# A Fourier filter and a mixture of experts on one core: rows due later, halves that go when their sums are made, w2 of the short tiles loaded along more tiles

## The chip, the cores and the metric

The kernel runs on one core of a Trainium2 chip. The metric is the device time of one execution in microseconds (us), as the median of several runs. A core has five engines, each with an instruction queue of its own: TensorE (PE in the profile) for matrix products, VectorE (DVE), ScalarE (ACT), GpSimd (POOL), and SyncE (SP), which here issues most DMA transfers. Every engine works through its own list in the order in which the program wrote it, and waits at an instruction whose input another engine or a transfer hasn't delivered.

## The reference

Two blocks, one after the other. The first filters every channel of a sequence in the frequency domain; the second sends each row to the one expert of eight that its gate prefers.

```python
# x: (8, 2496, 256); filt_r, filt_i: (1249, 256)
X = np.fft.rfft(x, axis=1)
y = np.fft.irfft(X * (filt_r + 1j * filt_i)[None], n=2496, axis=1)

x = y.reshape(19968, 256)
logits = x @ w_gate                        # (19968, 8)
expert = argmax(logits, axis=1)
gate = probability of that expert (softmax)
for e in range(8):                         # w1: (8, 256, 1024), w2: (8, 1024, 256)
    rows = rows whose expert is e
    out[rows] = gate[rows] * (relu(x[rows] @ w1[e]) @ w2[e])
```

## The kernel before

The Fourier transform of length 2496 = 39 x 64 is done as matrix products in four steps per batch (a and b forward, c and d back, with the filter between b and c). Between a and b the data goes through DRAM (`zd`), and between c and d again (`ud`). After d come the gate's logits, the routing, and a scatter of every row into a list of its expert in DRAM (`rows`). A tile of 512, 256 or 128 rows of one expert is then read back (`xg`), transposed (`xT`), multiplied by w1, passed through relu, multiplied by w2, scaled by the gate and scattered to the output.

The tiles of experts from earlier batches are worked on between the Fourier steps of later ones; after the last batch only expert tiles remain. Which step goes next is decided once, when the program is written, by a model of the time: `now` is TensorE's model time, `free` the time at which each other engine is thought free, `when` the time at which something is counted as there.

Loads are queued ahead:

```python
def prefetch():
    i = got["x"]
    if i < len(work) and rows_at[work[i][3]] <= now[0] and i - used["x"] < 2:
        rows_in(i)
        when["x", i] = now[0] + 6.0
        got["x"] += 1
    for what in ("w1", "w2"):
        h = got[what]
        if h < 2 * len(work) and rows_at[work[h // 2][3]] <= now[0] and (
                h - used[what] < ((3 if what == "w1" else 2) if h < 2 * SHORT else 8)):
            weights(h, what == "w2")
            when[what, h] = now[0] + 7.0
            got[what] += 1
    for h in range(used["w1"], got["w1"]):
        if quarters(h // 2) and h not in wsum and len(wsum) < 2 and when["w1", h] <= now[0]:
            w1_sums(h)
```

The first product of a tile (with w1) is done in two halves `h`. For tiles of 512 rows, and those of 256 rows of the last batch, a half is done with seven block products in place of eight, which need sums of blocks of the rows (`sums`, one set per tile) and of blocks of w1 (`wsum`, one set per half), both made by GpSimd:

```python
def turn_x(i):
    ...  # transposes of the rows, copies out of PSUM
    if quarters(i):
        ...  # four gpsimd.tensor_tensor over sums
        free["p"] = max(free["p"], now[0]) + 0.75 * n

def w1_sums(h):
    ...  # four gpsimd.tensor_tensor over wsum
    free["p"] = max(free["p"], now[0]) + 3.0

def hidden_by_quarters(h):
    ...
    q = product(w[:, 0, 0], b[:, 0, 0])      # no sums
    ...
    q = product(w[:, 1, 0], b[:, 1, 0])      # no sums
    add(hT[:, 0, :, 0], q, part)
    yield 1.71
    q = product(ws[:, 1], t[:, 1])           # sums of both kinds from here on
    ...
```

The steps of the expert tiles, each with its TensorE time and the thing it needs:

```python
def half(h):
    i, g = divmod(h, 2)
    n = TILES[i][0]
    if quarters(i):
        if h not in wsum:
            yield lambda: w1_sums(h), 0.0, ("w1", h)
        steps = hidden_by_quarters(h)
        for t in (1.71, 1.71, 1.71, 0.85):
            yield lambda: next(steps), t * n / 4, ("w1", h)
        wsum.pop(h)
    else:
        for a in range(4):
            yield lambda: hidden(i, g, a), 0.43 * n, ("w1", h)
    ...

def due(what, i):
    return when.get((what, i), now[0] + 1.0) <= now[0]

for i in range(NT):
    ahead = i > 0 and (used["x"] > i or due("x", i)) and due("w1", 2 * i)
    if i > 0 and not ahead:
        yield from results(i - 1)
    yield from turned(i)
    yield from half(2 * i)
    if i + 1 < NT and due("x", i + 1):
        yield from turned(i + 1)
    if ahead:
        yield from results(i - 1)
    yield from half(2 * i + 1)
```

And the loop that chooses between the next Fourier step `f` and the next expert step `e`:

```python
asked = e and e[2] in when
halt = f and f[2] and (f[2][0] in "uy" and held_y[0] == YB)
late_in = f and f[2] and lands.get(f[2], 0.0) > now[0]
if e and asked and (not f and not sides or
        when[e[2]] <= now[0] and (credit > 0.0 or not f or halt or late_in)):
    e[0]()                                   # the expert step
    ...
elif f and not halt and (not f[2] or f[2] == "y" or f[2] in ins):
    f[1]()                                   # the Fourier step
    ...
else:
    now[0] += 1.0
```

`late_in` says that the Fourier step's input is counted as still on its way; `f[2] in ins` only that its load has been queued.

The short tiles of 128 rows at the end take w2 of all eight experts from SBUF (`w2s`, 16 loads of 512 KB). `late` exists once the last Fourier step and the last routing are written:

```python
def weights(h, second):
    i, k = divmod(h, 2)
    if late and second and TILES[i][1] == B - 1 and late["n"] < 2 * E:
        e, hf = divmod(late["n"], 2)
        nc.sync.dma_start(out=late["w2s"][:, e, hf * FH2:(hf + 1) * FH2], in_=moe_w2[e, hf])
        late["n"] += 1
    if second and i >= SHORT:
        return
    ...  # the load of w1 or w2 of this tile
```

Of the kernel before, what the change touches and what calls it, by code (L numbers as in the profile page):

```python
# [22 lines left out]
E = 8  # L23
# [95 lines left out]
def kernel(  # L119
# [18 lines left out]
    B = x.shape[0]  # L138
# [73 lines left out]
    now = [0.0]  # L212
# [475 lines left out]
    late = {}  # L688
# [19 lines left out]
    def weights(h, second):  # L708

        i, k = divmod(h, 2)  # L710
        if late and second and TILES[i][1] == B - 1 and late["n"] < 2 * E:

            e, hf = divmod(late["n"], 2)
            nc.sync.dma_start(out=late["w2s"][:, e, hf * FH2:(hf + 1) * FH2], in_=moe_w2[e, hf])
# [3 lines that stand above are left out]
        ev = nc.sync.value_load(work[i][1], min_val=0, max_val=E - 1)  # L718
        if second:
            w2t[h] = pools["moe"].tile([P, FH2, D], F32, tag="w2t", name="w2t", bufs=2)  # L720
            nc.sync.dma_start(out=w2t[h], in_=moe_w2[bass.ds(ev, 1), k].rearrange("o p i d -> p (o i) d"))
        else:
            pool, bufs = (late["w1"], 8) if i >= SHORT else (pools["moe"], 3)
            w1t[h] = pool.tile([P, DH, 2, 2 * P], F32, tag="w1t", name="w1t", bufs=bufs)
            nc.sync.dma_start(out=w1t[h], in_=moe_w1[bass.ds(ev, 1), k].rearrange("o p i h f -> p (o i) h f"))

    def turn_x(i):
        n, xg = work[i][0], xgs.pop(i)
        idt[i] = pools["moe"].tile([P, 4, 1], I32, tag="idt", name="idt", bufs=3)
        gts[i] = pools["moe"].tile([P, 4, 1], F32, tag="gts", name="gts", bufs=3)  # L730
        nc.vector.tensor_copy(idt[i][:, :n], xg.bitcast(I32)[:, :n, D:D + 1])  # L731
        nc.vector.tensor_copy(gts[i][:, :n], xg[:, :n, D + 8:D + 9])
        xts[i] = pools["moe"].tile([P, DH, 4 * P], F32, tag="xT", name="xT", bufs=2)
        for dh in range(DH):
            pt = bank().rearrange("p (i q) -> p i q", i=4)
            for j in range(n):
                nc.tensor.transpose(pt[:, j, :], xg[:, j, dh * P:(dh + 1) * P], ident)  # L737
            evac(xts[i][:, dh, :n * P].rearrange("p (j q) -> p j q", j=n), pt[:, :n], n * P)
        if quarters(i):

            b = xts[i][:, :, :n * P].rearrange("p h (r c) -> p h r c", r=2)
            t = sums[i] = pools["moe"].tile([P, 4, 2 * P], F32, tag="sums", name="sums", bufs=2)[:, :, :n * HP]
            nc.gpsimd.tensor_tensor(t[:, 0], b[:, 0, 1], b[:, 0, 0], op=ALU.subtract)
            nc.gpsimd.tensor_tensor(t[:, 1], b[:, 1, 1], t[:, 0], op=ALU.subtract)
            nc.gpsimd.tensor_tensor(t[:, 2], b[:, 1, 1], b[:, 0, 1], op=ALU.subtract)
            nc.gpsimd.tensor_tensor(t[:, 3], b[:, 1, 0], t[:, 1], op=ALU.subtract)
            free["p"] = max(free["p"], now[0]) + 0.75 * n

    def w1_sums(h):

        w = w1t[h]
        t = wsum[h] = pools["moe"].tile([P, 4, 2 * P], F32, tag="wsum", name="wsum", bufs=2)
        nc.gpsimd.tensor_tensor(t[:, 0], w[:, 0, 1], w[:, 1, 1], op=ALU.add)  # L753
        nc.gpsimd.tensor_tensor(t[:, 1], t[:, 0], w[:, 0, 0], op=ALU.subtract)  # L754
        nc.gpsimd.tensor_tensor(t[:, 2], w[:, 0, 0], w[:, 0, 1], op=ALU.subtract)
        nc.gpsimd.tensor_tensor(t[:, 3], w[:, 1, 0], t[:, 1], op=ALU.subtract)
        free["p"] = max(free["p"], now[0]) + 3.0

    def hidden_by_quarters(h):

        i = h // 2
        w, ws, t = w1t[h], wsum[h], sums[i]
        n = work[i][0]
        b = xts[i][:, :, :n * P].rearrange("p h (r c) -> p h r c", r=2)
        hT = pools["moe"].tile([P, 2, 2, 4 * P], F32, tag="hT", name="hT", bufs=3)
        hs.setdefault(i, []).append(hT)  # L770
        hT = hT[:, :, :, :n * P].rearrange("p f v (r c) -> p f v r c", r=2)

        def product(left, right):
            q = bank()[:, :n * P].rearrange("p (v c) -> p v c", v=2)
            for v in range(2):
                mm(q[:, v], lhsT=left[:, v * P:(v + 1) * P], rhs=right, start=True, stop=True)  # L776
            return q

        def add(o, q, a):
            nc.vector.tensor_tensor(o, q, a, op=ALU.add)  # L780
            free["v"] = max(free["v"], now[0]) + 0.15 + 0.14 * n

        def relu(o, q):
            nc.scalar.activation(o.rearrange("p v r c -> p v (r c)"), q.rearrange("p v r c -> p v (r c)"), AF.Relu)  # L784
            free["s"] = max(free["s"], now[0]) + 0.2 + 0.22 * n

        low, part = hT[:, 1, :, 0], hT[:, 0, :, 1]
        q = product(w[:, 0, 0], b[:, 0, 0])
        nc.scalar.copy(out=part, in_=q)  # L789
        free["s"] = max(free["s"], now[0]) + 0.6  # L790
        q = product(w[:, 1, 0], b[:, 1, 0])
        add(hT[:, 0, :, 0], q, part)
        yield 1.71
        q = product(ws[:, 1], t[:, 1])
        add(part, q, part)
        q = product(ws[:, 2], t[:, 2])
        add(low, q, part)
        yield 1.71
        q = product(ws[:, 0], t[:, 0])
        add(hT[:, 1, :, 1], q, low)  # L800
        add(part, q, part)
        q = product(w[:, 1, 1], t[:, 3])
        add(low, q, low)
        relu(hT[:, 1], hT[:, 1])
        yield 1.71
        q = product(ws[:, 3], b[:, 1, 1])
        add(part, q, part)
        relu(hT[:, 0], hT[:, 0])
        yield 0.85
# [139 lines left out]
    def prefetch():  # L949

        i = got["x"]
        if i < len(work) and rows_at[work[i][3]] <= now[0] and i - used["x"] < 2:
            rows_in(i)
            when["x", i] = now[0] + 6.0
            got["x"] += 1
        for what in ("w1", "w2"):
            h = got[what]
# [9 lines that stand above are left out]
    def experts():  # L967

        def turned(i):
            if used["x"] == i:
                yield lambda: turn_x(i), 0.22 * TILES[i][0], ("x", i)
                used["x"] += 1
# [4 lines that stand above are left out]
            if quarters(i):  # L980
                if h not in wsum:
                    yield lambda: w1_sums(h), 0.0, ("w1", h)
                steps = hidden_by_quarters(h)
                for t in (1.71, 1.71, 1.71, 0.85):
                    yield lambda: next(steps), t * n / 4, ("w1", h)
                wsum.pop(h)
            else:
                for a in range(4):
                    yield lambda: hidden(i, g, a), 0.43 * n, ("w1", h)
            w1t.pop(h)  # L990
            used["w1"] += 1
            if g:
                xts.pop(i), sums.pop(i, None)

        def due(what, i):
            return when.get((what, i), now[0] + 1.0) <= now[0]

        def results(i):
            for j in range(TILES[i][0]):
                yield lambda: result(i, j), 3.42, ("w2", 2 * i + 1)  # L1000
            hs.pop(i), idt.pop(i), gts.pop(i), w2t.pop(2 * i, None), w2t.pop(2 * i + 1, None)
            used["w2"] += 2
# [12 lines that stand above are left out]
        yield from results(NT - 1)  # L1015
# [77 lines left out]
```

## Time and profile before

| | |
|---|---|
| time, median of 3 runs | 1587.04 us (1583.56 to 1589.24) |
| span of the profiled run | 1582.1 us, mean granted TensorE clock 0.989 |
| VectorE, ScalarE, GpSimd busy | 47%, 33%, 42% of the span |
| moved by DMA | 287.55 MB, 182 GB/s over the span |
| chain that ended last | TensorE 71%, DMA 11%, issue 8%, VectorE 4%, GpSimd 4% |
| w1 loads (512 KB), issue to landing | 3.7 us median, 130 of them |
| w2 loads (512 KB), issue to landing | 4.2 us median, 84 of them |
| Fourier inputs from `zd` (256 KB) | 9.2 us median, 70 of them |

In the profile L776 is the product by quarters (`product`), L817 the plain first product (`hidden`), L834 the second product (`result`), L737 the transposes of the rows (`turn_x`). L337, L351, L372 and L391 are the Fourier steps a, b, c and d, L358 to L362 the filter on VectorE between b and c, L743 to L746 the sums of the rows and L753 to L756 those of w1. `fin` is any Fourier input, `bank` a PSUM bank. A line of the waits names the engine, what it was about to do, what it waited for, the total in us, how often, and the longest. The profile's slices are 40 equal parts of the span, with the busy share in tenths.

### The profile page before, as it was taken

What the parts mean: (1) busy time and instruction counts of PE and PEld (TensorE: products, weight loads), DVE (VectorE), ACT (ScalarE), POOL (GpSimd) and SP (SyncE); (2) the same over time, 40 slices, a digit from 0 to 9 for tenths busy, and PEclk for the clock granted to TensorE, in tenths of its full rate; (3) what the DMA queues carried; (4) which work ended last, traced back from release to release, by engine and by line L of the source; (5) the groups of instructions that cost most, each with busy time, mean ns of one, the idle gap of its engine ahead of it and who ended that gap; (6) DMA issues with size and microseconds to landing.
All of it is one profiled execution on the core that took longest, in us unless ns stands there. A gap on an engine that the chain in (4) does not pass through costs nothing.

```text
span 1582.1 us, 24007 instructions
## 1 busy us (share of the span) xinstructions
PE 1519.9 (96%) x7624; PEld 1207.6 (76%) x7624; DVE 748.4 (47%) x1923; ACT 524.1 (33%) x1074; POOL 669.5 (42%) x817
## 2 busy tenths in 40 slices
PE   7989797999989999999999999999999999989998
PEld 5534456767668868787688788888888898989997
DVE  4675574544745565456645455564343434420000
ACT  4434342333333233233233332322232323223433
POOL 4132135324544454365345636646455546621111
PEclk9999898999999999999999999999999999999999
DMA  8669796697675477365733734443345456565560
GB/s 244 167 189 274 251 299 221 183 313 234 200 240 154 162 224 213 104 178 149 201 109 127 214 104 121 128 146 124 116 170 172 151 172 227 184 234 178 175 186 32
DMA packets 119281, 287.55 MB, mean 182 GB/s; under 512 B 17587, under 2 KB 58812, under 8 KB 119157
## 3 DMA queue, kind: packets, MB, share of 16 engines
q1 hardware_dynamic: 99941, 242.69, 51.3%
q0 software_dynamic: 19216, 43.33, 7.8%
q8 instruction: 63, 1.03, 0.3%
q14 instruction: 61, 0.50, 0.1%
HBM read 205.95 MB, written 80.90 MB: 181 GB/s over the span
## 4 chain that ended last, share of the span: by engine, by line
PE 71%; DMA 11%; issue 8%; DVE 4%; POOL 4%; ACT 1%; POOLq 0%; SPq 0%; ACTq 0%; DVEq 0%
PE bank L834 28%; PE bank L776 20%; DMA out_dram<-ys,idt 6%; PE bank L391 4%; PE bank L351 3%; PE bank L372 3%; PE bank L337 3%; PE bank L817 3%; DMA zd<-zo 2%; PE bank L466 2%; PE bank L737 2%; PE lt L480 1%; DVE hT L780 1%; DMA fin<-ud 1%; PE bank L413 1%
## 5 line engine op out<-in xcount | busy, mean ns | idle before, releaser
L834 PE MATMUL bank<-w2t,hT 128*128 128x256 f32 x2240 | 500.9, 381 | 5.4 <-DMA w2t<-in_moe_w_dram 4.3
L834 PEld LDWEIGHTS bank<-w2t,hT 128*128 128x128 f32 x2240 | 422.3, 191 | 78.6 <-issue 18.6
L780 DVE TENSOR_TENSOR hT<-bank,hT 128x512 f32<-128x512 f32 (+1 forms) x504 | 299.1, 626 | 287.2 <-PE bank L776 202.9
L840 POOL DMA_INDIRECT out_dram<-ys,idt x163 | 161.7, 992 | 505.0 <-ACT ys L839 242.0
L607 POOL DMA_INDIRECT rows<-yo,row x176 | 174.4, 991 | 178.0 <-DVE row L577 47.2
L784 ACT ACTIVATE hT<-hT 128x1024 f32<-128x1024 f32 (+1 forms) x144 | 133.0, 957 | 339.6 <-DVE hT L780 339.6
L839 ACT ACTIVATE ys<-bank,gts 128x256 f32<-128x256 f32 x159 | 75.2, 475 | 416.4 <-PE bank L834 361.3
L776 PE MATMUL bank<-sums,wsum 128*128 128x256 f32 (+1 forms) x864 | 186.7, 363 | 11.2 <-POOL wsum L754 8.3
L776 PEld LDWEIGHTS bank<-sums,wsum 128*128 128x128 f32 x864 | 151.3, 194 | 40.7 <-POOL wsum L754 10.1
L817 PE MATMUL bank<-xT,w1t 128*128 128x128 f32 (+1 forms) x928 | 134.5, 299 | 2.3 <-ACT zo L227 1.4
L817 PEld LDWEIGHTS bank<-xT,w1t 128*128 128x128 f32 x928 | 123.0, 193 | 18.0 <-issue 8.2
L776 PE MATMUL bank<-xT,w1t 128*128 128x256 f32 (+1 forms) x576 | 123.2, 357 | 0.0
L776 PEld LDWEIGHTS bank<-xT,w1t 128*128 128x128 f32 x576 | 100.7, 190 | 16.2 <-issue 4.1
L731 DVE COPY idt<-xg 128x4 int32<-128x4 int32 (+2 forms) x65 | 19.3, 297 | 176.2 <-DMA out_dram<-ys,idt 143.0
L753 POOL TENSOR_TENSOR wsum<-w1t 128x256 f32<-128x256 f32 x73 | 53.7, 735 | 111.2 <-PE bank L776 90.6
L358 DVE TENSOR_TENSOR ys<-bank,ht 128x512 f32<-128x512 f32 x80 | 54.9, 686 | 91.7 <-PE bank L351 91.3
L823 ACT ACTIVATE hT<-bank 128x128 f32<-128x128 f32 (+1 forms) x230 | 68.0, 299 | 52.1 <-PE bank L817 46.4
L834 PE MATMUL bank<-w2s,hT 128*128 x368 | 83.2, 379 | 0.0
L372 PE MATMUL bank<-ys,tcs 128*128 128x512 f32 x140 | 75.2, 620 | 8.1 <-DVE ys L362 7.9
L337 PE MATMUL bank<-fin,tas 117*120 117x512 f32 x154 | 75.1, 606 | 0.4 <-ACT hT L789 0.4
L834 PEld LDWEIGHTS bank<-w2s,hT 128*128 128x128 f32 x368 | 68.1, 190 | 8.3
L351 PE MATMUL bank<-fin,tbs 128*128 128x512 f32 x140 | 73.1, 603 | 0.0
(149 smaller groups left out, 1754.9 us busy)
## 6 DMA issues: line engine op xcount, KB each, us to landing
w1t<-in_moe_w_dram SPq DMA_DIRECT2D x130, 512.0 KB, 3.7
w2t<-in_moe_w_dram SPq DMA_DIRECT2D x84, 512.0 KB, 4.2
fin<-in_x_dram SPq DMA_DIRECT2D x40, 512.0 KB, 9.4
fin<-zd SPq DMA_DIRECT2D x70, 256.0 KB, 9.2
ud<-uo SPq DMA_DIRECT2D x70, 256.0 KB, 4.6
zd<-zo SPq DMA_DIRECT2D x35, 480.0 KB, 10.1
fin<-ud SPq DMA_DIRECT2D x35, 480.0 KB, 9.6
xg<-rows SPq DMA_DIRECT2D x28, 544.0 KB, 3.6
```

Source lines behind the costliest of these rows:

```text
L337: mm(p[:TK, :], lhsT=tas, rhs=xt[:TP, j:j + 2, :], start=True, stop=True)
L351: mm(p, lhsT=tbs, rhs=zi[:, j:j + 2, :], start=True, stop=True)
L372: mm(p, lhsT=tcs, rhs=ys, start=True, stop=True)
L607: sc = nc.gpsimd.indirect_dma_start(out=rowsd, out_offset=bass.IndirectOffsetOnAxis(ap=at, axis=0), in_=what, in_offset=None,)
L776: mm(q[:, v], lhsT=left[:, v * P:(v + 1) * P], rhs=right, start=True, stop=True)
L780: nc.vector.tensor_tensor(o, q, a, op=ALU.add)
L784: nc.scalar.activation(o.rearrange("p v r c -> p v (r c)"), q.rearrange("p v r c -> p v (r c)"), AF.Relu)
L817: mm(p[:, :m], lhsT=w1t[2 * i + g][:, dh, fh, v * P:(v + 1) * P], rhs=xts[i][:, dh, :m], start=(dh == 0), stop=(dh == DH - 1))
L823: lambda: nc.scalar.activation(hT, p[:, :m], AF.Relu))
L834: mm(p[:, :D], lhsT=hs[i][k % 4 // 2][:, k // 4, k % 2, j * P:(j + 1) * P], rhs=w2, start=(k == 0), stop=(k == FT - 1))
L839: lambda: nc.scalar.activation(ys, p[:, :D], AF.Copy, scale=gate))
L840: nc.gpsimd.indirect_dma_start(out=out, out_offset=bass.IndirectOffsetOnAxis(ap=idt[i].bitcast(U32)[:, j, :], axis=0), in_=ys, in_offset=None,
```

## The change

Four numbers and conditions of the model change; no operation is added or removed. Rows are counted as there 9 us after their load is queued and not 6, so later than w1 with its 7. The sums of rows and of w1 get a time at which they are counted as made (`when["sums", i]`, `when["wsum", h]`), and all steps of a half by quarters wait in the model for both, where they waited for w1 alone. And the loads of `w2s` go along with the w2 loads of any tile once `late` exists, not only those of the last batch, so that they are spread over an earlier stretch. The aim is an order in which TensorE does not come to an operand before it is there.

```diff
-        if late and second and TILES[i][1] == B - 1 and late["n"] < 2 * E:
+        if late and second and late["n"] < 2 * E:
...
-            free["p"] = max(free["p"], now[0]) + 0.75 * n
+            free["p"] = max(free["p"], now[0] + 1.0) + 0.75 * n
+            when["sums", i] = free["p"] + 1.0
... (w1_sums)
         free["p"] = max(free["p"], now[0]) + 3.0
+        when["wsum", h] = free["p"] + 1.0
... (prefetch)
-            when["x", i] = now[0] + 6.0
+            when["x", i] = now[0] + 9.0
... (half)
+                when["quarters", h] = max(when["sums", i], when["wsum", h])
                 steps = hidden_by_quarters(h)
                 for t in (1.71, 1.71, 1.71, 0.85):
-                    yield lambda: next(steps), t * n / 4, ("w1", h)
+                    yield lambda: next(steps), t * n / 4, ("quarters", h)
```

## The prediction

> **What bounds the kernel now.** I read the totals first, then the busy shares by slice, then the list of what TensorE waited for, and last the timelines around the longest waits.
>
> ```profile
> span 1582.1 us, 24007 instructions
> PE 1519.9 (96%) x7624; PEld 1207.6 (76%) x7624; DVE 748.4 (47%) x1923; ACT 524.1 (33%) x1074; POOL 669.5 (42%) x817
> PE   7989797999989999999999999999999999989998
> PEclk9999898999999999999999999999999999999999
> ```
>
> TensorE is the bound: 96% busy, nobody else over half. The change adds and removes no matmul, so only TensorE's idle time (1582.1 - 1519.9 = 62 us) and its half-rate clock can give anything. Both sit in the first quarter. The waits of TensorE name what stops it:
>
> ```profile
> PE bank L737 <- DMA xg<-rows: 9.6, 2, 5.6
> PE bank L776 <- POOL wsum L754: 8.3, 2, 5.1
> PE bank L372 <- DVE ys L362: 7.9, 7, 3.6
> ...
> PE bank L834 <- DMA w2t<-in_moe_w_dram: 4.3, 2, 3.4
> ```
>
> The change is aimed at four of these: rows 9.6, weight sums 8.3, row sums (further down the list) 1.8, w2 4.3, together 24.0 us. In time they are: rows 5.6 us at 172.7 to 178.3 (first 256-row tile) and 4.0 us at 452.5; weight sums at 242 and 257 (first 512-row tile); row sums at 1342 and 1357; w2 at 1388 to 1394. The timeline of TensorE at the weight sums (the bracket is the idle time before a group):
>
> ```profile
> 240.37 1.99 PE L776 MATMUL bank<-xT,w1t 128*128 128x256 f32 x8
> 247.49 5.34 PE L776 MATMUL bank<-sums,wsum 128*128 128x256 f32 x12 [5.13 <-POOL wsum L754]
> ...
> 259.93 4.26 PE L776 MATMUL bank<-sums,wsum 128*128 128x256 f32 x12 [3.19 <-POOL wsum L754]
> ...
> 265.75 3.62 PE L817 MATMUL bank<-xT,w1t 128*128 128x256 f32 x16
> ```
>
> and the queue of SyncE beside it:
>
> ```profile
> 234.38 0.38 SPq L698 DMA_DIRECT2D xg<-rows  x1
> ...
> 241.78 1.00 SPq L300 DMA_DIRECT2D zd<-zo  x2
> 247.56 0.47 SPq L322 DMA_DIRECT2D fin<-zd  x1
> 248.09 0.59 SPq L323 DMA_DIRECT2D fin<-zd  x1
> 248.73 1.06 SPq L317 DMA_DIRECT2D fin<-in_x_dram  x2
> ```
>
> While the expert tile ran badly (240 to 266), the next batch's Fourier inputs were still on their way: fin<-zd is issued only at 247.56, after six expert loads and after the zd write has landed. The clock by stretch shows what a wait costs afterwards (columns: stretch, length, busy times, clock, DMA share, GB/s):
>
> ```profile
> 165.00:185.00 20.00, 12.95 (x59) 7.99 (x58) 10.43 (x30) 5.25 (x13) 7.90 (x8) 0.77 0.90 303
> 245.00:255.00 10.00, 7.51 (x25) 6.24 (x26) 6.51 (x13) 0.20 (x1) 8.60 (x11) 0.66 0.75 231
> 255.00:265.00 10.00, 6.80 (x26) 5.45 (x25) 3.35 (x8) 2.82 (x5) 5.98 (x8) 0.83 0.70 249
> 450.00:460.00 10.00, 5.99 (x22) 4.15 (x21) 4.48 (x9) 4.20 (x7) 2.06 (x4) 0.87 1.02 324
> ```
>
> **What the Trainium skill says.** "TensorE: Matmul & The Clock Gate", Part 1, has the array drop to half rate after an idle window of about 3.4 us and stay there until it has been busy for such a window. The trace agrees: the clock is below 1.00 only in stretches with waits, and 20 product matmuls at 259.93 take 5.99 us in the chain against 4.32 elsewhere. "Perfetto Trace Analysis", Tensor Engine Instruction, says that TensorE may pull weight loads ahead but not matmuls; so a matmul whose input is late stops everything behind it, as at 242 to 247 here. "DMA: Bandwidth & Descriptors", Anatomy of one DMA, says that a wait on a semaphore happens at the issuing sequencer: an issue that waits holds up all later ones. Agreed: a semaphore wait of 4.7 us stands on SyncE directly before the fin<-zd issue at 247.56.
>
> **The change part by part.** Durations at full clock, from the timelines: a 512-wide Fourier product (two records) 0.86 us, a 256-column expert product (two records) 0.43, a transpose 0.11, a w2 tile result of 16 records 3.45. With them I added up, from the changed program's order of instructions, how much TensorE work lies between the point where a load is queued and its first use.
>
> *Rows counted due 3 us later, first tile.* The work between load and transposes grows from 7.0 to 9.5 us: two inverse products and six logit products now stand before the tile. At 172.6 TensorE then does these 2.7 us instead of idling; but each waits for VectorE's filter chain (done at 174.6 and 177.4 in the timeline), so TensorE comes to the rows at 178.3, just when they land. The 2.7 us of work is done in dead time: -2.7. With shorter gaps some of the half-rate stretch goes: -1.
>
> *Rows at 452.5.* The lead was 6.9 us; in the new order no rows after the second site have less than 10.9 us, which is what was needed (6.9 + 4.0). The wait goes, and with it the half-rate 32 result matmuls behind it (8.52 us from start to start against 6.91): -4.0 - 1.6 = -5.6.
>
> *The half goes when its sums are made.* At the first 512-row tile TensorE took 265.75 - 240.37 = 25.4 us for 56 product records and 4 transposes, 56 x 0.216 + 0.44 = 12.5 us of work: 12.8 us lost. In the new order the sums have over 8 us of lead, so the GpSimd wait goes. But what fills the place? Before the transposes come two forward products, a rank, an inverse product and four transposes (3.5 us, inputs present), then the 8 transposes (0.9), two inverse products, logits, and at about 238.98 + 8 = 247 the first product of the next batch, whose input fin<-zd is the one issued at 247.56 and 248.09 with 9.2 us to landing: 257.3. The scheduler knows that it is late, but with the half not yet due it emits the Fourier step all the same. So a DMA wait of about 10.3 us takes the place of 8.3 us of GpSimd waits, with some 2 us of half-rate work behind it: 12.3 against 12.8, worth -0.5. This is the place where I chose: the queue ahead of that load is the same, word for word, in both programs, so I take its landing as unchanged.
>
> *w2 of short tiles earlier.* The 16 loads of 512 KB begin three tiles of 512 rows sooner and are out of all but two of the nine 256-row tiles. There every tile moves w1, w2 and rows in 13.6 us, and TensorE did not wait for them until the sums at 1342 and 1357 (1.8 us), where GpSimd came late after scatters that take up to 6.9 us to land against 2.4 on an idle queue. I give it -1. The 4.3 us for w2 at 1388 to 1394 stay: there seven w1 loads of the short tiles stand around two w2 loads in the queue, in the same order as before.
>
> *New small waits.* In the third quarter of the Fourier phase one inverse product now follows its forward product with a single product of 0.86 us between; VectorE's chain is four operations of 0.69, some 2.8: +2.2 with the latency.
>
> Sum: -2.7 - 1.0 - 5.6 - 0.5 - 1.0 + 2.2 = -8.6; from 1587 that is 1578.4, and I say 1579.
>
> **Rivals.** (a) All aimed waits but w2 go and nothing replaces them: 9.6 + 8.3 + 1.8 = 19.7 us and about 9 us of half rate, so 1558. For it: there are Fourier steps to fill with. Against it: the fill at 247 has no input. (b) The new wait for fin<-zd is longer than what it replaces, since everything behind a blocked matmul is late, the zd and ud stores that feed later loads too: another stall of the same kind at each batch would make 1595. Against it: from the second batch on, no Fourier input has a shorter lead than the 10.7 us that passed without a wait before. (c) Nothing moves: TensorE is busy 96%, the waits shift about, 1587. (d) The w2 loads at the 512-row tiles collide with the last Fourier loads: they start only after these have ended, so I give it little.
>
> **Range and chances.** The three runs of before spread by 5.7 us. The two largest terms, 5.6 at 452 and the 12 that are swapped at 247, are each uncertain by some 6: with the rest that makes 1568 to 1590. 2% would be 1555 or 1619; the first needs more than rival (a), the second three stalls like that at 247.
>
> **What would show it.** Right: the list of TensorE's waits has no POOL wsum line, less than 3 us for xg<-rows, and a new line L351 <- DMA fin<-zd of 8 to 12 us at about 247; the clock dips after it and no longer at 452; w2t stays at about 4 us. Wrong: no fin<-zd line (then rival a, nearer 1565), or several such lines over the batches (rival b).

## The result and the profile after

The changed kernel takes 1574.0 us (median of 4 runs, 1571.5 to 1576.8), the kernel before beside it 1587.3: ratio 0.992, 95% interval 0.989 to 0.995, or some 13 us of 1587. The prediction was 1579, from 1568 to 1590.

The totals and the busy shares by slice of the changed kernel:

```profile
span 1575.0 us, 23997 instructions
...
PE 1519.9 (97%) x7624; PEld 1206.2 (77%) x7624; DVE 746.5 (47%) x1923; ACT 524.5 (33%) x1074; POOL 665.8 (42%) x813
...
PE   7988898999999999999999999999999999999998
...
PEclk9998999999999999999999999999999999999999
```

TensorE is busy for the same 1519.9 us as before, and idle for 55 where it was idle for 62. The two profiled runs differ by 7.1 us and the medians by 13.3, so the profiles show the places rather than the whole size. The list of what TensorE waited for (total us, how often, longest) in the changed kernel, where the second product is now L836 and the product by quarters L778:

```profile
PE bank L372 <- DVE ys L362: 11.8, 9, 3.6
PE bank L372 <- DVE gts L732: 6.0, 1, 6.0
...
PE bank L836 <- DMA w2t<-in_moe_w_dram: 2.1, 2, 1.3
...
PE bank L391 <- ACT zo L227: 1.5, 1, 1.5
```

The lines for rows (9.6 before), for the sums of w1 (8.3) and for the sums of rows (1.8) are gone. In their place stand one wait of 6.0 for VectorE and two more of the small ones for the filter's `ys` (11.8 against 7.9). The first place to look at is the first 512-row tile, where the prediction put a wait for `fin<-zd`. TensorE's timeline there, idle time in brackets:

```profile
241.37 1.03 PE L351 MATMUL bank<-fin,tbs 128*128 128x512 f32 x2
...
243.11 1.08 PE L372 MATMUL bank<-ys,tcs 128*128 128x512 f32 x2
244.12 1.00 PE L480 MATMUL lt<-yt,wg 128*32 128x234 f32 x12
251.09 2.05 PE L372 MATMUL bank<-ys,tcs 128*128 128x512 f32 x2 [5.97 <-DVE gts L732]
252.93 0.56 PE L491 MATMUL bank<-ident,ls 96*117 96x96 f32 x2
253.29 1.53 PE L351 MATMUL bank<-fin,tbs 128*128 128x512 f32 x2
256.35 1.95 PE L337 MATMUL bank<-fin,tas 117*120 117x512 f32 x4 [1.53 <-DMA fin<-in_x_dram]
```

There is a stall, 7.5 us with the 1.5 us after it where 10.3 was foreseen, but it stands at the inverse product L372 and not at the forward product L351. When L351 comes at 253.29 it doesn't wait: `fin<-zd`, issued at 247.1 and 247.7, has landed within some 6 us. The stall is for VectorE's filter. The label `gts L732` is only the last small copy behind it in VectorE's list; the filter itself ends at 250.9. VectorE's timeline says why:

```profile
243.57 0.74 DVE L554 COPY yo<-sd 117x32 f32<-117x32 f32 x1
...
245.25 0.56 DVE L565 TENSOR_TENSOR pos<-run,rks 117x64 f32<-117x64 f32 x1
245.84 0.65 DVE L566 TENSOR_TENSOR pos<-pos,rks 117x64 f32<-117x64 f32 x1
246.42 0.70 DVE L569 TENSOR_TENSOR bs<-cnt,eoff 117x8 f32<-117x8 f32 x1
...
248.13 0.68 DVE L358 TENSOR_TENSOR ys<-bank,ht 128x512 f32<-128x512 f32 x1
...
250.25 0.69 DVE L362 TENSOR_TENSOR ys<-ys,yw 128x512 f32<-128x512 f32 x1
```

The forward product had been in PSUM since about 242.4 (241.37 + 1.03), but the routing of the batch (L541 to L578, 242.88 to 248.2) stood ahead of the filter (L358) in VectorE's list. The clock by stretch (columns: stretch, length, busy times of TensorE, weight loads, VectorE, ScalarE and GpSimd, clock, DMA share, GB/s):

```profile
165.00:185.00 20.00, 15.64 (x76) 7.17 (x75) 14.51 (x55) 8.57 (x20) 6.90 (x7) 0.91 0.78 255
245.00:255.00 10.00, 3.85 (x9) 1.57 (x6) 5.97 (x17) 1.04 (x3) 7.12 (x9) 0.66 0.74 214
...
430.00:440.00 10.00, 8.10 (x31) 4.55 (x29) 4.14 (x7) 2.45 (x5) 3.23 (x4) 1.00 1.05 326
440.00:450.00 10.00, 8.15 (x31) 6.10 (x32) 7.64 (x28) 3.28 (x6) 2.92 (x4) 0.94 1.04 297
```

At the first tile (165 to 185) TensorE is busy for 2.7 us more than before and the clock rises from 0.77 to 0.91. TensorE's timeline from the last forward product (L351) ahead of the tile to its transposes (L737), before:

```profile
171.73 1.03 PE L351 MATMUL bank<-fin,tbs 128*128 128x512 f32 x2
178.33 1.08 PE L737 MATMUL bank<-ident,xg 128*128 128x128 f32 x4 [5.57 <-DMA xg<-rows]
```

and in the changed kernel:

```profile
175.40 1.03 PE L351 MATMUL bank<-fin,tbs 128*128 128x512 f32 x2
178.41 1.31 PE L372 MATMUL bank<-ys,tcs 128*128 128x512 f32 x2 [1.98 <-DVE ys L362]
...
182.91 0.60 PE L737 MATMUL bank<-ident,xg 128*128 128x128 f32 x4
```

Up to that L351 the order is the same in both, and here TensorE comes to it 3.7 us later, so a part of the shorter wait is not the new order's. At 430 to 450, just ahead of where the second rows wait was, TensorE is idle for 3.8 of 20 us (0.4 before).

To compare programs of different order I counted how much full-clock work TensorE has done at each moment (each matmul by the distance between starts at full clock that the timelines show for its shape) and read off how far it had fallen behind that work. What is lost within a stretch of work, in us, in six profiles:

| work done (and what lies there) | before | w2 part alone | whole change | change without w2 part | rows part alone | sums part alone |
|---|---|---|---|---|---|---|
| 131-150 (first 256-row tile) | 10.1 | 13.6 | 6.0 | 10.2 | 11.4 | 11.6 |
| 185-230 (first 512-row tile) | 13.3 | 13.5 | 10.3 | 9.9 | 11.1 | 11.4 |
| 230-300 | 3.3 | 3.1 | 1.1 | 0.1 | 1.0 | 0.2 |
| 300-385 (rows at 452 before) | 8.4 | 8.2 | 9.3 | 8.1 | 7.6 | 9.0 |
| 665-725 | 4.3 | 3.7 | 5.3 | 5.3 | 1.3 | 2.2 |
| 1250-1305 (last long tiles) | 7.4 | 3.3 | 2.8 | 2.8 | 6.9 | 6.8 |

In columns one and two TensorE's order is the same, and in three and four too, so their differences (3.5 and 4.2 us in the first row) show how far one profile can be trusted for one stretch.

### The profile page after: what moved, and what is told of

It reads as the page before. It is cut to its first block, busy times and chain, and to the rows that moved or that the text cites. A ratio compares the mean times of both kernels' runs of the same rounds, so it can differ in the third digit from the quotient of the medians.

```text
span 1575.0 us, 23997 instructions
## 1 busy us (share of the span) xinstructions
PE 1519.9 (97%) x7624; PEld 1206.2 (77%) x7624; DVE 746.5 (47%) x1923; ACT 524.5 (33%) x1074; POOL 665.8 (42%) x813
## 3 DMA queue, kind: packets, MB, share of 16 engines
q8 instruction: 63, 1.03, 0.3%
## 4 chain that ended last, share of the span: by engine, by line
PE 78%; DMA 8%; issue 8%; DVE 5%; ACT 1%; POOL 0%; SPq 0%; POOLq 0%; DVEq 0%; ACTq 0%
PE bank L836 30%; PE bank L778 22%; PE bank L391 4%; DMA out_dram<-ys,idt 4%; PE bank L337 3%; PE bank L351 3%; PE bank L372 3%; PE bank L819 3%; PE bank L466 2%; PE bank L737 2%; PE lt L480 1%; DMA zd<-zo 1%; DVE hT L782 1%; PE bank L413 1%; DMA fin<-in_x_dram 1%
## 5 line engine op out<-in xcount | busy, mean ns | idle before, releaser
L836 PE MATMUL bank<-w2t,hT 128*128 128x256 f32 x2240 | 499.5, 380 | 4.9 <-DMA w2t<-in_moe_w_dram 2.1
L836 PEld LDWEIGHTS bank<-w2t,hT 128*128 128x128 f32 x2240 | 421.3, 190 | 77.9 <-issue 15.8
L778 PE MATMUL bank<-sums,wsum 128*128 128x256 f32 (+1 forms) x864 | 182.2, 357 | 0.0
L778 PEld LDWEIGHTS bank<-sums,wsum 128*128 128x128 f32 x864 | 149.1, 190 | 26.4 <-issue 10.1
L778 PE MATMUL bank<-xT,w1t 128*128 128x256 f32 (+1 forms) x576 | 123.0, 356 | 0.4 <-ACT uo L227 0.4
L778 PEld LDWEIGHTS bank<-xT,w1t 128*128 128x128 f32 x576 | 100.7, 190 | 16.6 <-issue 4.2
L372 PE MATMUL bank<-ys,tcs 128*128 128x512 f32 x140 | 77.5, 636 | 17.8 <-DVE ys L362 11.8
L358 DVE TENSOR_TENSOR ys<-bank,ht 128x512 f32<-128x512 f32 x80 | 54.8, 685 | 64.5 <-PE bank L351 64.0
L836 PE MATMUL bank<-w2s,hT 128*128 x368 | 83.2, 379 | 0.0
L836 PEld LDWEIGHTS bank<-w2s,hT 128*128 128x128 f32 x368 | 68.1, 190 | 8.3
L351 PE MATMUL bank<-fin,tbs 128*128 128x512 f32 x140 | 73.3, 607 | 0.0
## 6 DMA issues: line engine op xcount, KB each, us to landing
zd<-zo SPq DMA_DIRECT2D x35, 480.0 KB, 11.8
```

The costliest lines, as they stand in the source:

```text
L351: mm(p, lhsT=tbs, rhs=zi[:, j:j + 2, :], start=True, stop=True)
L372: mm(p, lhsT=tcs, rhs=ys, start=True, stop=True)
L836: mm(p[:, :D], lhsT=hs[i][k % 4 // 2][:, k // 4, k % 2, j * P:(j + 1) * P], rhs=w2, start=(k == 0), stop=(k == FT - 1))
```

## The experiments

Times are ratios to the kernel before, run beside on the same chip; the chips differ by 1%, so only ratios are compared across the three groups. Differences in us are these ratios' distance from 1 times the time before (1586.6 us in the first group).

**Each part alone, and the change without its w2 part.** The first keeps before's order on TensorE and moves only the queue of loads:

```diff
-        if late and second and TILES[i][1] == B - 1 and late["n"] < 2 * E:
+        if late and second and late["n"] < 2 * E:
```

> The w2 part alone; TensorE's order is that of before, word for word, only SyncE's queue differs. Theory A (the three parts act each in its own place; the w2 part is worth the 4.7 us by which the changed kernel gains on TensorE between 1336 and 1404): 1582.5 us, no POOL sums wait in the last 300 us, w2t wait about 2 us in place of 4.3. Rival B (the loads of w2s cost nothing where they were; the tail differed by the chance of one profile): 1587 us, and the waits of 1.8 and 4.3 us stay.

Measured: 0.9981 (0.9970 to 0.9992), 3.0 us faster, nearer to theory A, and with its signs: the w2t wait is 1.9 us, and no wait for `sums` is left at the end. The second only counts rows as due later:

```diff
-            when["x", i] = now[0] + 6.0
+            when["x", i] = now[0] + 9.0
```

> Rows counted due at 9 and not 6, alone. Theory A: the first 256-row tile is as in the changed kernel (its order there is the same), so 4 us less; at the first 512-row tile the transposes move behind the rank and stand right before the first product, so of 8.3 us of GpSimd waits 2 to 4 stay; rows at 452 don't wait. Sum: 1579 us. Rival C (it is the sums rule that does the work, rows are worth the 4 us alone): 1583 us, with over 6 us of POOL waits.

Measured: 0.9949 (0.9931 to 0.9968), 8.1 us faster, the time of theory A. The wait at 452 is gone and one GpSimd wait of 4.8 us for the sums of w1 is left, but the first 256-row tile still waits 4.6 us for its rows. The third has only the rule on sums:

```diff
-            free["p"] = max(free["p"], now[0]) + 0.75 * n
+            free["p"] = max(free["p"], now[0] + 1.0) + 0.75 * n
+            when["sums", i] = free["p"] + 1.0
...
+        when["wsum", h] = free["p"] + 1.0
...
+                when["quarters", h] = max(when["sums", i], when["wsum", h])
...
-                    yield lambda: next(steps), t * n / 4, ("w1", h)
+                    yield lambda: next(steps), t * n / 4, ("quarters", h)
```

> The half that waits for its sums, alone. Theory A: the first 256-row tile waits for rows as before (5.6 us); the GpSimd wait of 8.3 us at 242 to 260 goes and a wait for the Fourier input or for VectorE of 5 to 8 us takes its place: 1584 us. Rival C (the rule is the bulk of the gain): 1578 us.

Measured: 0.9965 (0.9952 to 0.9977), 5.6 us faster, midway between A and C. The GpSimd wait is gone, and a wait of 6.8 us for VectorE's filter stands in its place, as A said. The fourth is the change with the w2 condition put back; TensorE's order is that of the whole change:

> The change without its w2 part; TensorE's order is that of the changed kernel, word for word. Theory A: 1574.0 + 4.7 = 1578.7 us, with a POOL sums wait near 1340 and 4 us of w2t wait back. Rival B: 1574 us.

Measured: 0.9923 (0.9896 to 0.9950), 12.2 us faster, which is the whole change's gain (12.7) within the intervals. So the rows and the sums carry it: 8.1 and 5.6 alone, 12.2 together. The prediction gave the sums part 0.5 us, for the first 512-row tile alone. By the table the part alone gains there (11.4 against 13.4), between 230 and 300 (0.2 against 3.2) and at 665 to 725 (2.2 against 4.0).

**The w2 part on top, again.** On another chip, beside the whole change:

> The change without its part on the short tiles' w2, once more, beside the whole change on the same chip. Theory A (the part is worth something on top of the other two): 2 us or more slower than the changed kernel. Theory B (nothing on top): within 1.5 us of it.

> The changed kernel itself, for a time on the same chip as the next three. If the ratio of the first measurement, 0.992, holds, 0.992 times the kernel before.

Measured: 0.9895 (0.9879 to 0.9911) without it and 0.9898 (0.9869 to 0.9928) with it. Theory B held twice. The stretch 1250-1305 is 2.8 us in both profiles of the whole change, but 2.8 and 7.2 in the two profiles without the w2 part. The times don't show the difference; with these intervals a gain of 2 or 3 us can't be ruled out.

**Expert loads of a new batch behind its Fourier loads.** In all the orders above TensorE loses 10 us or more at the first 512-row tile. Was it that seven expert loads stood ahead of `fin<-zd` in SyncE's queue? In the changed kernel:

```diff
-            rows_at[b] = free["p"] + 4.0
+            rows_at[b] = free["p"] + 8.0
```

> The changed kernel, in which the expert loads of a new batch (rows, w1, w2) may be queued 8 us after the model's time of the last scatter and no longer 4 us, so that at the first tiles of 256 and 512 rows the stores to zd and the loads fin<-zd, fin<-x stand ahead of them in SyncE's queue. Theory Q (SyncE's queue, one list in order, is what makes TensorE's operands late there): most of the 5.7 us lost at 172 to 185 and of the 10.1 us at 236 to 262 goes, 1565 us, and TensorE's longest waits there fall below 2 us. Rival R (the stretch is short of work or of data in any order, and waits only change their names, as they did in the change itself): 1574, with a wait of about 6 us of another name at about 250.

Measured: 0.9953 (0.9936 to 0.9971), some 9 us slower than the change on that chip, so neither theory had the time. `fin<-zd` is now issued at 244.97, with the new batch's expert loads behind it, and TensorE loses 12.5 us in the stretch 185-230 all the same, against 9.8 in the change's profile on that chip. No wait stands out; what it waited for from 234 to 265:

```profile
PE bank L372 <- DVE ys L362: 3.0, 2, 1.8
PE lt L480 <- ACT yt L227: 1.5, 1, 1.5
PE bank L737 <- issue: 1.4, 1, 1.4
PE bank L372 <- issue: 0.7, 1, 0.7
PE rk L538 <- ACT ls L227: 0.5, 1, 0.5
PE bank L491 <- issue: 0.5, 1, 0.5
```

It is a chain of short steps from one engine to the next, forward product, filter, inverse product, logits, routing, without a ready expert tile to fill in. At the first tile (131-150) the loss is 13.8 us against 7.4, with a wait of 4.8 us for `fin<-ud` that the change doesn't have. The queue theory fell for this place; of rival R the kind held, waits of other names, but they are many small ones and not one of 6 us.

**Loads of w2 later.** At 452 the rows wait went, but the stretch 300-385 kept its loss. The changed kernel's list of waits for 425 to 462 shows something that the prediction had not looked for:

```profile
DVE zo L227 <- DMA zd<-zo: 6.9, 1, 6.9
...
ACT zo L227 <- DMA zd<-zo: 5.6, 1, 5.6
```

VectorE and ScalarE both stand still until 435.83, with a copy into a buffer of the ring of four that `zo` and `uo` share, because its store has not landed; the DMA engines are full (share 1.05). Ahead of that burst SyncE waits 8.4 us at a w2 load whose buffer TensorE still uses. Three kernels tried whether that block is the cause. First a rule for all long tiles, which lets the scheduler choose its order anew:

```diff
+            if i < SHORT and not late:
+                freed["w2"] = now[0] + 7.0
... (prefetch: a load only once freed[what] <= now[0])
```

> The changed kernel, in which a load of w2 of the long tiles is queued 7 us of model time after the last product that uses its buffer is written, and not at once. In the changed kernel SyncE stands 8.4 us at such a load at 398 to 406, waiting for TensorE to free the buffer, with the ud stores and the Fourier loads behind it; after that the DMA engines are full from 412 to 450, both zo copies wait 6 us for a buffer whose store hasn't landed, and TensorE loses 6 us at 430 to 450. Theory Q (the block in SyncE's queue is what bunches the transfers): those 6 us go, 1568 us, and SyncE's waits at L721 (50.7 us between 150 and 700) fall below 15. Rival R (the DMA engines are full there because of the bytes alone): the zo copies still wait some 5 us, 1574.

> Both of the edits before on top of the changed kernel. Theory Q: the gains add, 1559 us (six less for w2, nine less for the expert loads of a new batch). Rival R: 1574, within the run-to-run spread of the changed kernel.

Measured: 1.0224 (1.0171 to 1.0277), and 1.0153 (1.0089 to 1.0217) with both edits. SyncE's waits at L721 between 150 and 700 fell from 50.7 to 8.4 us as expected, but TensorE waits 15.4 us for w2 and steps move everywhere. Too much moves at once to blame one thing. So next with the order of TensorE kept as it is, and only the queue of SyncE changed; first for one tile:

```diff
-                weights(h, what == "w2")
+                if what == "w2" and 0 < h < 2 * SHORT and not late and h // 2 == 7:
+                    put_off.append((now[0] + 8.0, h))
+                else:
+                    weights(h, what == "w2")
```

> The changed kernel with one thing moved: the two w2 loads of the eighth tile, at which SyncE stands 8.4 us at 398 to 406 until TensorE frees their buffers, are queued behind the eleven stores and Fourier loads that followed them. The order of TensorE's and ScalarE's instructions is the same. Theory Q (that block bunches the transfers, and the bunching makes the zo copies wait for buffers): the stores and loads start some 8 us earlier, the 6 us waits of the zo copies at 429 to 436 shrink below 2 us and TensorE's loss at 430 to 450 from 6 us below 2, so 4 to 5 us faster than the changed kernel. Rival R (the DMA engines are full for their bytes' sake): the zo copies still wait some 5 us, within 1.5 us of the changed kernel.

Measured: 0.9885 (0.9870 to 0.9900) against 0.9898 for the change: within the intervals the same, as rival R said. The zo copies wait 3.3 and 2.9 us, in place of 4.8 and 4.1 in the change's profile on that chip, and the stretch 300-385 loses 9.6 us against 7.5 (1.7 us of that is the clock: 16 matmuls of the second product take 5.3 us from 405.1 on, where they take 3.6 in the change). The trace shows why theory Q was wrong. ScalarE's timeline in this kernel:

```profile
415.93 0.59 ACT L227 COPY uo<-bank 128x512 f32<-128x512 f32 x1 [0.38 <-PE bank L372]
```

and SyncE's:

```profile
416.55 1.09 SPq L300 DMA_DIRECT2D ud<-uo  x2
422.14 0.40 SPq L329 DMA_DIRECT2D fin<-ud  x1
```

The ud store that stood behind the two loads goes 0.03 us after its own source is there (415.93 + 0.59 = 416.52). In the change's profile on that chip, with the block, it is the same, 0.03 us from the end of the copy (407.16 + 0.59 = 407.75) to the store (ScalarE's timeline, then SyncE's):

```profile
407.16 0.59 ACT L227 COPY uo<-bank 128x512 f32<-128x512 f32 x1 [0.38 <-PE bank L372]
...
407.78 1.10 SPq L300 DMA_DIRECT2D ud<-uo  x2
```

In both, TensorE makes that source after 32 matmuls of the second product. SyncE would have stood at the store if it had not stood at the w2 load. The burst of transfers starts when TensorE's order lets it.

Then for all long tiles from the fifth on, 5 us later:

> The same for every long tile from the fifth on: its w2 loads are queued 5 us of model time later, the order of TensorE's instructions the same. Theory Q: the 50.7 us that SyncE stands at w2 loads between 150 and 700 fall below 15, and with them the loss at 430 to 450 and some of the 10 us that TensorE loses in small waits from 460 to 1060: 6 us or more faster than the changed kernel. Rival R: within 1.5 us. Rival S (the w2 loads come too late in their turn): waits for w2t of 2 us or more at the last Fourier steps and a slower kernel.

Measured: 1.0000 (0.9984 to 1.0016); the whole gain is gone, about 16 us against the change. One line of TensorE's waits tells it:

```profile
PE bank L836 <- DMA w2t<-in_moe_w_dram: 14.7, 3, 11.4
```

and SyncE's timeline ahead of the longest of them:

```profile
880.47 0.34 SPq L721 DMA_DIRECT2D w2t<-in_moe_w_dram  x1
888.25 1.08 SPq L300 DMA_DIRECT2D ud<-uo  x2
893.29 5.52 SPq L329 DMA_DIRECT2D fin<-ud  x7
899.91 0.37 SPq L721 DMA_DIRECT2D w2t<-in_moe_w_dram  x1
```

The second half of w2 now stands behind a ud store, which waits for TensorE, and behind the loads of what that store writes, which wait for it to land. It is issued 19.4 us after the first half, and TensorE stands for 11.4 us. That is rival S. SyncE's waits between 150 and 700 only changed places: at w2 loads they fell from 50.0 us in the change on that chip to 22.4, at stores of `uo`, whose source comes from ScalarE, they rose from 32.5 to 76.1. A w2 load early in the queue blocks nothing that could go; a w2 load behind a store is itself blocked.

**w1 of the short tiles held back.** For the w2 wait at about 1388:

```diff
+            if what == "w1" and h >= 2 * SHORT and got["w2"] < 2 * SHORT:
+                continue
```

> The changed kernel, in which no w1 load of the short tiles is queued before the last w2 load of the long tiles. Theory G (the w2 wait at about 1388 comes from the w1 loads that stand around the w2 loads in the queue): TensorE's wait L836 for w2t, 2.1 us in the changed kernel and 4.3 in the kernel before, goes to 0, 1572 us. Rival H (the wait is for the buffer or for the transfer time of w2 itself, or a w1 wait of the short tiles takes its place): 1574 or more, with a w2t or w1t wait of 2 us or more after 1380.

Measured: 0.9901 (0.9872 to 0.9929), against 0.9898 for the change on that chip. The list of TensorE's waits has no w2t line any more, and TensorE's order is that of the change until after its place; so theory G had the cause right: the w1 loads around it. In the time it doesn't show; 2 us are within these intervals.

None of these versions beats the change by more than its measurement is uncertain.

## Why the prediction was right or wrong

The time is within the range, 5 us below the figure. Step by step:

- **First tile, -2.7 and -1.0: right in kind, the size uncertain.** 10.1 us of loss became 6.0, and the clock rose. But TensorE came to the tile's place 3.7 us later than before, so the rows had more time to land. Over the three profiles of each order here (that of before in columns one, two and six) the means are 11.8 and 9.2, 2.6 us apart where 3.7 was predicted, and profiles of one order differ by up to 5.4 us. The rows wait is 0 in the change, 1.9 in the change without its w2 part and 4.6 in the rows part alone.
- **Rows at 452.5, "the wait goes, and with it the half-rate 32 result matmuls": failed.** The rows wait went, and 32 result matmuls take 6.91 us again (457.01 to 463.92); but the loss from work 300 to 385 was 8.4 us and is 9.3. Its place took 1.5 us for `zo`, 1.5 for VectorE's `hT`, small waits for ScalarE and a dip of the clock (0.89 at 450 to 460). The step looked at the lead of one load and not at what else was short: the DMA engines are full there before (1.02) and after (1.05). In the six profiles of the table the stretch loses 7.6 to 9.3 us, with the rows wait and without. Why it loses that much in every order is not settled; that SyncE's block is not the cause is shown.
- **First 512-row tile, "a DMA wait of about 10.3 us takes the place of 8.3 us of GpSimd waits": the swap was right, its cause and size wrong.** No wait for `fin<-zd` came up. The transfer landed in some 6 us at most, where I took the median of 9.2 (the loads ahead of it are seven, not six), and TensorE was late for it, since VectorE's routing held up the inverse product by 6.0 us. Loss 13.3 became 10.3: -3.0 in place of -0.5. The prediction followed TensorE's inputs through DMA and not through VectorE's list.
- **What was missed: work 230 to 300.** 3.3 us of loss became 1.1 (0.1 without the w2 part); among them is a wait of 1.4 us for ScalarE's `zo` at 331 before. Each of the two main parts alone does it too.
- **New waits behind the filter, +2.2: right.** Between work 665 and 675 the loss is 2.7 us where there was none, and in no profile of a part alone is it over 0.3. From 675 to 725 1.6 are given back, for a net +1.0.
- **w2 of the short tiles, -1, and "the 4.3 us for w2 stay": too small in this pair.** The stretch went from 7.4 to 2.8, the w2t wait from 4.3 to 2.1. The part alone is worth 3.0 us in the time; on top of the others nothing that the runs can show. What goes with the part is the wait for `sums` after 1310: it is in four of the five profiles without the part (0.9 to 2.4 us) and in none of the nine with it. The w2t wait does not go with it: 0.8 to 4.3 us without the part, up to 3.3 with it.

The rows of the table add up to -12.0 for the change, and the medians differ by 13; but these two profiles differ by 7.1. Most of the rest, 3.7 us, was lost ahead of the first tile, where the order is the same in both. That the predicted sum came near the time is in part luck: its largest term, -5.6 at 452, brought nothing, and what it lacked elsewhere (-3.0 for -0.5, -2.2 for nothing, -4.6 for -1 in this pair) filled the place. Rival (a) of the prediction, 1558, failed for the reason given there: other waits moved into the gaps, though not the one that was named. Of the signs of being right, two came (no wsum line, no rows wait over 3 us), and three did not (the `fin<-zd` line, no dip behind 452, w2t at 4). The sign of being wrong, no `fin<-zd` line, came too; the time then named for it, 1565, did not.

## What to carry to other kernels

When a wait is removed by putting other steps ahead, follow each of these steps' inputs through every engine that makes them, its list in order included, and not only through the transfers. Ask of each stretch how much it loses in any order: two of the gaps here kept some 8 to 13 us in all six profiles of the table, and only the names of the waits changed. A queue that stands at one entry costs something only if an entry behind it could have gone; look at when that entry's own source was ready.

## What the runs showed of the hardware

VectorE's operations on two operands in SBUF often take much longer beside GpSimd's tensor operations, and those that read PSUM don't. GpSimd's timeline in the changed kernel beside the slow operations at 243 to 247:

```profile
243.54 0.73 POOL L743 TENSOR_TENSOR sums<-xT 128x256 f32<-128x256 f32 x1 [1.13 <-ACT xT L227]
```

Over four profiles (before, the change, the change and the change without its w2 part on the second chip, 150 to 640 us), medians of single operations without and with such a GpSimd operation beside them (5 to 24 cases with it):

| operation on VectorE | operands | without | with |
|---|---|---|---|
| L569, 117x8 | both SBUF | 0.16 | 0.70 |
| L565, 117x64 | both SBUF | 0.22 | 0.58 |
| L362, 128x512 | both SBUF | 0.69 | 1.03 |
| L358, 128x512 | one PSUM | 0.68 | 0.69 |
| L574, reduction of 117x64 | one SBUF | 0.27 | 0.27 |

The Trainium skill, "SBUF — State Buffer", Who interferes with whom, says that the two engines share one pair of SBUF ports under an exclusive lock, and that a VectorE operation with two SBUF inputs contends for it with a GpSimd operation that reads SBUF. The trace agrees, L569 with its 0.70 beside a GpSimd operation of 0.72 above all. In the stall at 245 to 251 the five slow routing operations (0.74, 0.71, 0.56, 0.65, 0.70 against 0.18, 0.18, 0.22, 0.23, 0.16 without) cost 2.4 of the 6.0 us by this count. The first two are L554, a copy with a single operand in SBUF: in the same four profiles it takes 0.18 in the median beside GpSimd and 0.74 at worst.

The kernel with `rows_at` 8 us later is a test of this count. There the same routing runs with no GpSimd sums beside it (they begin at 261.42), and VectorE's timeline has

```profile
246.75 0.18 DVE L554 COPY yo<-sd 117x32 f32<-117x32 f32 x1
...
247.33 0.23 DVE L565 TENSOR_TENSOR pos<-run,rks 117x64 f32<-117x64 f32 x1
247.59 0.23 DVE L566 TENSOR_TENSOR pos<-pos,rks 117x64 f32<-117x64 f32 x1
247.74 0.16 DVE L569 TENSOR_TENSOR bs<-cnt,eoff 117x8 f32<-117x8 f32 x1
```

The routing (L541 to L578) takes 2.95 us, from 246.05 to 249.00, where it takes 5.33 in the changed kernel, and the inverse product behind it waits 1.8 us and not 6.0 (TensorE's order differs there). So the routing is 2.4 us longer beside the sums. That is no gain of the kernel yet: this one loses 12.5 us at that place, most of it in other waits, and none was run that moves the sums alone.
